# A partial 512-column unit across two steps, a weight tile's preparation moved later, and the sums of one more step by VectorE

## The chip, the core and the metric

One core of one Trainium2 chip. The metric is the device time of one execution in microseconds (us); 503.96 us is the median of three before the change. In what follows PE is TensorE, ACT is ScalarE, DVE is VectorE.

## What is computed

Attention with capped scores over 4 batches, 12 heads, 448 tokens, 64 features, then a layer with three weight matrices, an elementwise maximum and an output matrix:

```python
scores = cap * np.tanh(scale * (q @ k.T) / cap)
attn = exp(scores - max); attn = attn / (sum(attn) + 1e-09)
x = (attn @ v)                       # 1792 tokens x 768 features
h = max(max(x @ w1, x @ w2), x @ w3)
out = h @ w_out
```

All in float32. The weights arrive as 64-bit numbers and are turned into two float32r parts on the chip.

## The kernel before

**Attention.** Twelve groups of four heads, one for each step t = 0 to 11. A group has seven key chunks j. For each, PE computes `scores(t, j)` (L133, eight instructions on 64 x 64 quarters of the array), ACT applies `tanh` (L139) and `expo` (L142), and PE accumulates `values(t, j)` in the tile `av` (L151, also 64 x 64 quarters). Scores alternate between two tiles `qk`. Steps 0 to 3 are `early_step`; steps 4 to 11 are `step`; a thirteenth call ends group 11. Each engine runs its list in the order in which the functions issue it.

**Sums.** DVE adds the seven exponentials: `add` (into `s_t`), `add_aside` (chunks 3, 4 and 5 into `p_t`), `add_both`, and `add(t, 6)` at the step's end. For groups 5 to 11 (`BY_DVE`) the next step begins with `quarter_sums`: a DVE transpose (L185) and a reduction (L186) into `g_um`, then `join_sums` (L191), eight tiny PE instructions that add the parts of `g_um` by the pattern `pat`. For group 4, `sums` (L178) does the whole sum on PE instead. Then `recip` (reciprocal L199 or L202, transpose L203), `normalize` and `split_x` on DVE make the two float32r parts of x in `xx`.

**Units.** The layer's products are cut into units (n, b): weight tile n (768 x 128, six row parts `kc`) by token block b. Block 0 has 256 columns, blocks 1 to 3 have 512. A unit is 18 matmuls (L273 to L275, three for each row part) on the whole 128 x 128 array. Steps 4 to 11 take one unit each (`FILL`), in bank 0 of the tile `sm`; `empty` writes it to its place: tile 0 of a feature block by an ACT copy (L286), the others by a DVE maximum. Units of 256 columns stand in steps 4 to 6, of 512 in steps 7 to 11. All the others follow in `mlp` after attention, where PE runs products alone.

**Weights.** A weight tile is prepared by `conv(n, 0..5)` (L246 to L266), mostly on DVE; `CONV` and `PLACES` say in which step and where in it. Tile 2's pieces 3 and 4 stand at the end of step 4, piece 5 in step 5; tile 3's piece 0 is done by ACT at the end of step 7 (`SCALED`).

**One step on PE**, in order: sums or join of the group before among the first scores and values; `scores(t, 4)`, `values(t-1, 6)`, `scores(t, 5)`, the unit's products, `scores(t, 6)`, `values(t, 0)`, `values(t, 1)`, `scores(t+1, 0)`, `values(t, 2)`, `scores(t+1, 1)`, `values(t, 3)`, `scores(t+1, 2)`, and in the next step `scores(t+1, 3)`, `values(t, 4)`, `values(t, 5)`, `join_sums`. On ACT the end of a step is `tanh(t, 6)`, `expo(t, 5)` where the unit has 256 columns and `expo(t, 5)`, `tanh(t, 6)` where it has 512; then `expo(t, 6)`, the copy or ACT piece if there is one, and `tanh(t+1, 0)`.

Of the kernel before, what the change touches and what calls it, by code (L numbers as in the profile page):

```python
# [11 lines left out]
ALU = mybir.AluOpType  # L12
# [5 lines left out]
KC = DM // 128  # L18
NJ = S // 64
GB = H // 4  # L20
NG = B * GB
# [8 lines left out]
CAP_LO = 1e-6  # L30
WARM = 7

FILL = {4 + i: (i % 3, i // 3) for i in range(8)}
FILLED = (2, 2)
BY_PE = (0, 1, 2, 3)
BY_DVE = (5, 6, 7, 8, 9, 10, 11)
CONV = {0: [(0, 0), (0, 1), (0, 2), (0, 3), (0, 4), (0, 5), (1, 0), (1, 1), (1, 2), (1, 3), (1, 4)], 1: [(1, 5)],
        2: [(2, 0), (2, 1)], 3: [(2, 2)], 4: [(2, 3), (2, 4)], 5: [(2, 5)], 8: [(3, 1)], 9: [(3, 2)], 10: [(3, 3)]}
PLACES = {0: (0, 0, 0, 0, 1, 1, 1, 3, 3, 5, 5), 5: (4,), 8: (4,), 9: (4,), 10: (4,)}
EARLY = 4  # L40
SCALED = {7: 3}
LOADS = {1: 2, 6: 3, 11: 4}


# [1 line left out]
def attn_max_mlp_kernel(ctx: ExitStack, tc: tile.TileContext, first, q, k, v, wts, out):  # L46
# [11 lines left out]
    def tl(name, shape, dt=F32, pool=const):  # L58
        return pool.tile(shape, dt, name=name, tag=name)
# [4 lines left out]
    acap, sc_t, eps_f, eps_g, fl = (tl(n, [128, 1]) for n in ("acap", "sc_t", "eps_f", "eps_g", "fl"))  # L64
    fl_i = tl("fl_i", [128, 1], I32)
    ones = tl("ones", [128, 64])
    pat = tl("pat", [128, 64])
    pat_i = tl("pat_i", [128, 64], I32)
    wz = tl("wz", [128, S], F32R)

# [39 lines left out]
    def rows(i):  # L110
        return slice(64 * i, 64 * i + 64)
# [17 lines left out]
    def scores(t, j):  # L129
        ps = slot(t, j)  # L130
        for R in range(2):
            for s in range(2):
                nc.tensor.matmul(  # L133
                    ps[rows(s), R, 0:S], k_t[t % 2][rows(R), j, s, :], q_t[t % 2][rows(R), s, :],
                    start=True, stop=True, skip_group_check=True,
                )

    def tanh(t, j):
        nc.scalar.activation(out=e_of(t, j), in_=slot(t, j)[:, :, 0:S], func=AF.Tanh, scale=sc_t)  # L139

    def expo(t, j):
        nc.scalar.activation(out=e_of(t, j), in_=e_of(t, j), func=AF.Exp, scale=acap)  # L142
# [13 lines left out]
    def add(t, j, eps=None):  # L156
        s = flat(s_t[t % 2])
        if j == 1:
            nc.vector.scalar_tensor_tensor(
                out=s, in0=flat(e_of(t, 0)), scalar=eps, in1=flat(e_of(t, 1)), op0=ALU.add, op1=ALU.add  # L160
            )
        else:
            tt(nc.vector, s, s, flat(e_of(t, j)), ALU.add)
# [24 lines left out]
    def join_sums():  # L188
        for s in range(2):
            for R in range(2):  # L190
                nc.tensor.matmul(  # L191
                    sm[rows(R), s, 0:QB], pat[rows(s), :], g_um[rows(s), R * QB:R * QB + QB],
                    start=True, stop=True, skip_group_check=True,
                )

    def recip(t, by_dve=False):
        x, r = x_t[t % 2], r_t[t % 2]
        if by_dve:
            nc.vector.reciprocal(r.rearrange("p (a b) -> p a b", a=2), sm[:, :, 0:QB])  # L199
        else:  # L200
            nc.vector.transpose(out=x, in_=sm[:, :, 0:S])
            nc.vector.reciprocal(r, flat(x).rearrange("p (a b) -> p a b", b=32)[:, :, 0])  # L202
        nc.vector.transpose(  # L203
            out=flat(x).rearrange("p (a b) -> p a b", b=32), in_=r.unsqueeze(2).to_broadcast([128, 2 * QB, 32])
        )
# [62 lines left out]
    def products(n, b, ps, kcs):  # L268
        at = slice(*BLOCKS[b])
        ps = ps[:, 0:at.stop - at.start]  # L270
        for kc in kcs:
            w_h, w_l, a_h, a_l = wh[n % 3][:, kc, :], wl[n % 3][:, kc, :], xx[:, 0, kc, at], xx[:, 1, kc, at]
            nc.tensor.matmul(ps, w_h, a_h, start=(kc == 0), stop=False)  # L273
            nc.tensor.matmul(ps, w_h, a_l, start=False, stop=False)  # L274
            nc.tensor.matmul(ps, w_l, a_h, start=False, stop=(kc == KC - 1))  # L275
# [94 lines left out]
    def step(t, eps, ahead):  # L370
        last = t - 1
        if t < NG - 1:
            load_qk(t + 1)
        by_dve = last in BY_DVE
        if by_dve:
            quarter_sums(last)
        else:
            sums(last, last in BY_PE)
            recip(last)
        if t == NG:  # L380
            for j in range(4, NJ):
                values(last, j)
            ahead(range(3))
            join_sums()
            recip(last, True)
            normalize(last)
            split_x(last)
            return
        n, b = FILL[t]
        tanh(t, 1)  # L390
        expo(t, 0)
        scores(t, 3)
        if t > EARLY:
            values(last, 4)
        values(last, 5)
        if by_dve:
            join_sums()
            recip(last, True)
        tanh(t, 2)
        expo(t, 1)  # L400
        add(t, 1, eps)
        scores(t, 4)
        values(last, 6)
        normalize(last)
        tanh(t, 3)
        expo(t, 2)
        add(t, 2)
        split_x(last)
        loads(t)
        scores(t, 5)  # L410
        products(n, b, sm[:, 0, :], range(KC))
        tanh(t, 4)
        expo(t, 3)
        tanh(t, 5)
        expo(t, 4)
        add_aside(t, 4)
        scores(t, 6)
        if b:
            expo(t, 5)
            tanh(t, 6)  # L420
        else:
            tanh(t, 6)
            expo(t, 5)
        if n:
            empty(n, b, sm[:, 0, :])
        convert(t, 4)
        add_aside(t, 5)
        add_both(t)
        if not n and not b:
            empty(n, b, sm[:, 0, :])  # L430
        expo(t, 6)
        if not n and b:
            empty(n, b, sm[:, 0, :])
        if t in SCALED:
            conv(SCALED[t], 0, True)
        values(t, 0)
        values(t, 1)
        if t + 1 < NG:
            scores(t + 1, 0)
        values(t, 2)  # L440
        if t + 1 < NG:
            scores(t + 1, 1)
        if t not in BY_PE:
            add(t, 6)
        convert(t, 5)
        values(t, 3)
        if t + 1 < NG:
            tanh(t + 1, 0)
            scores(t + 1, 2)
# [77 lines left out]
    with tc.manual_schedule():  # L527
        nc.sync.dma_start(out=k_t[0][:, 0:2].rearrange("p a b c -> p (a b c)"), in_=k[0, :, 0:256])
        nc.scalar.dma_start(out=q_0[:, 0:2 * S + 1], in_=first)
        nc.scalar.dma_start(out=k_t[0][:, 2:].rearrange("p a b c -> p (a b c)"), in_=k[0, :, 256:])  # L530
        conv_load(0, nc.scalar)
        load_v(0, nc.scalar)
        conv_load(1, nc.scalar)
        nc.vector.memset(wz.bitcast(F32), 0.0)
        for _ in range(WARM):
            nc.tensor.matmul(sm[:, 0, 0:S], wz[:, 0:128], wz, start=True, stop=True)
        nc.gpsimd.memset(ones, 1.0)
        nc.gpsimd.memset(eps_g, 1e-9 / 64.0)
        nc.gpsimd.iota(pat_i, pattern=[[1, 64]], base=128, channel_multiplier=-1)
        nc.vector.tensor_single_scalar(pat_i, pat_i, 31, op=ALU.bitwise_and)  # L540
        nc.vector.tensor_single_scalar(pat, pat_i, 0, op=ALU.is_equal)
        nc.scalar.activation(out=acap, in_=cap_t, func=AF.Abs)
        nc.vector.tensor_scalar(out=fl, in0=acap, scalar1=CAP_HI, scalar2=None, op0=ALU.is_le)
        nc.vector.scalar_tensor_tensor(
            out=fl_i, in0=acap, scalar=CAP_LO, in1=fl, op0=ALU.is_ge, op1=ALU.mult
        )
        nc.vector.reciprocal(sc_t, acap)
        nc.vector.tensor_scalar_mul(sc_t, sc_t, 1.0 / float(D) ** 0.5)
        nc.scalar.activation(out=eps_f, in_=acap, func=AF.Exp, scale=-1.0)
        nc.vector.tensor_scalar_mul(eps_f, eps_f, 1e-9 / 64.0)  # L550
        scores(0, 0)
        scores(0, 1)
        tanh(0, 0)
        scores(0, 2)
        flag = nc.values_load(fl_i[0:1, 0:1], min_val=0, max_val=1)
        with tc.If(flag > 0) as br:
            load_qk(1)
            load_v(1)
            for t in range(NG + 1):
                if t < EARLY:  # L560
                    early_step(t, eps_f)
                else:
                    step(t, eps_f, lambda kcs: products(*FILLED, banks[0], kcs))
            mlp({*FILL.values()}, convs)
        outs[0] = 0
        with br.Else():
            general_attention()
            for n in range(3):
                for i in range(6):
                    conv(n, i)  # L570
                conv_load(n + 2)
            for i in range(4):
                conv(3, i)
            mlp(set(), convs)
# [49 lines left out]
```

## Time and profile before

| | |
|---|---|
| median of three executions | 503.96 us (503.28 to 504.41) |
| the profiled execution | 504.0 us, its span 502.2 us |
| mean granted TensorE clock | 0.995 |
| busy PE, DVE, ACT | 490.6, 266.4, 226.0 us |
| attention | to about 178 us of the span |

The span runs from the first to the last instruction; 1.8 us lie around it. A matmul's recorded duration overlaps the next one, so that on PE the distance from start to start is what counts.

### The profile page before, as it was taken

How to read it: one execution, taken by the hardware profiler on the slowest of the kernel's cores; microseconds unless marked ns; L12 is line 12 of the kernel's file. 1: busy time of each engine (PE TensorE's matmuls, PEld its weight loads, DVE VectorE, ACT ScalarE, POOL GpSimd, SP SyncE). 2: the span in 40 equal slices, each digit the busy share in tenths (PEclk: the TensorE clock that was granted, in tenths of full speed). 3: DMA queues.
4: the chain of work that ended last, by engine and by line, in shares of the span. 5: the costliest groups of instructions: out<-in, count | busy, mean ns of one | idle time of the engine just before them, and what ended most of it. 6: DMA issues, size and time to landing. Idle time of an engine off the chain costs nothing.

```text
span 502.2 us, 7429 instructions
## 1 busy us (share of the span) xinstructions
PE 490.6 (98%) x3207; PEld 350.1 (70%) x3207; DVE 266.4 (53%) x330; ACT 226.0 (45%) x273; POOL 0.6 (0%) x7
## 2 busy tenths in 40 slices
PE   6999999999999999999999999999999999999994
PEld 2333344454545588888888888888888888888883
DVE  4999999997898946143233323423432585222000
ACT  6999999989988602210210221121011553222110
POOL 0000000000000000000000000000000000000000
PEclk9999999999999999999999999999999999999998
DMA  8243333531324001111101301111030102233111
GB/s 331 88 174 112 112 111 111 174 104 45 111 81 158 1 0 64 63 64 63 64 5 59 125 1 63 64 63 38 27 125 1 63 2 101 89 135 127 62 74 48
DMA packets 12423, 41.44 MB, mean 83 GB/s; under 512 B 1376, under 2 KB 2528, under 8 KB 12384
## 3 DMA queue, kind: packets, MB, share of 16 engines
q1 hardware_dynamic: 11520, 37.95, 21.9%
q10 hardware_dynamic: 864, 2.95, 1.5%
q8 instruction: 27, 0.44, 0.3%
q14 instruction: 12, 0.10, 0.1%
HBM read 35.39 MB, written 5.51 MB: 81 GB/s over the span
## 4 chain that ended last, share of the span: by engine, by line
PE 85%; DVE 6%; ACT 5%; issue 2%; DMA 1%; DVEq 0%
PE qk L273 9%; PE qk L274 9%; PE qk L275 9%; PE qk L133 8%; PE sm L273 8%; PE av L151 8%; PE sm L274 7%; PE sm L275 7%; PE av L273 6%; PE av L275 6%; PE av L274 6%; ACT e_all L139 3%; DVE s_t L108 2%; ACT e_all L142 1%; ACT e_all L146 1%
## 5 line engine op out<-in xcount | busy, mean ns | idle before, releaser
L273 PE MATMUL qk<-xx,wh 128*128 128x512 f32 (+1 forms) x264 | 89.9, 340 | 0.0
L274 PE MATMUL qk<-xx,wh 128*128 128x512 f32 (+1 forms) x264 | 89.8, 340 | 0.0
L275 PE MATMUL qk<-xx,wl 128*128 128x512 f32 (+1 forms) x264 | 89.5, 339 | 0.0
L139 ACT ACTIVATE e_all<-qk,sc_t 128x896 f32<-128x896 f32 x84 | 83.6, 1014 | 11.1 <-PE qk L133 11.1
L133 PE MATMUL qk<-q,k_t 64*64 64x448 f32 x672 | 77.5, 547 | 2.7 <-ACT e_all L139 2.2
L151 PE MATMUL av<-e_all,v_t 64*64 64x448 f32 x672 | 72.7, 536 | 0.0
L262 ACT CAST wh<-cw 128x768 fp32r<-128x768 f32 x21 | 17.6, 836 | 116.2 <-DVE cw L258 116.2
L273 PE MATMUL sm<-xx,wh 128*128 128x512 f32 (+1 forms) x180 | 69.2, 384 | 0.0
L274 PE MATMUL sm<-xx,wh 128*128 128x512 f32 (+1 forms) x180 | 68.4, 380 | 0.0
L275 PE MATMUL sm<-xx,wl 128*128 128x512 f32 (+1 forms) x180 | 68.2, 379 | 0.0
L142 ACT ACTIVATE e_all<-e_all,acap 128x896 f32<-128x896 f32 x60 | 62.0, 1047 | 0.2
L273 PEld LDWEIGHTS qk<-xx,wh 128*128 128x128 f32 x264 | 50.2, 190 | 6.3 <-issue 0.7
L275 PEld LDWEIGHTS qk<-xx,wl 128*128 128x128 f32 x264 | 50.1, 190 | 5.6
L274 PEld LDWEIGHTS qk<-xx,wh 128*128 128x128 f32 x264 | 50.2, 190 | 5.3
L151 PEld LDWEIGHTS av<-e_all,v_t 64*64 64x64 f32 x672 | 25.9, 133 | 37.2 <-issue 34.1
L275 PE MATMUL av<-xx,wl 128*128 128x512 f32 x132 | 51.4, 390 | 0.0
L273 PE MATMUL av<-xx,wh 128*128 128x512 f32 x132 | 51.4, 390 | 0.0
L274 PE MATMUL av<-xx,wh 128*128 128x512 f32 x132 | 51.4, 390 | 0.0
L133 PEld LDWEIGHTS qk<-q,k_t 64*64 64x64 f32 x672 | 23.8, 134 | 38.5 <-issue 17.7
L108 DVE TENSOR_TENSOR wl<-cw,wh 128x768 fp32r<-128x768 f32 x24 | 22.9, 956 | 41.6 <-ACT wh L262 36.2
L273 PEld LDWEIGHTS sm<-xx,wh 128*128 128x128 f32 x180 | 33.8, 188 | 11.8 <-DVE x_t L203 4.2
L108 DVE TENSOR_TENSOR e_all<-e_all,qk 128x256 f32<-128x256 f32 (+1 forms) x20 | 11.1, 555 | 52.7 <-PE qk L275 52.7
(77 smaller groups left out, 486.1 us busy)
## 6 DMA issues: line engine op xcount, KB each, us to landing
wd<-in_wts_dram SPq DMA_DIRECT2D x22, 768.0 KB, 4.2
k_t<-in_k_dram SPq DMA_DIRECT2D x11, 448.0 KB, 3.4
q<-in_q_dram SPq DMA_DIRECT2D x11, 448.0 KB, 5.0
v_t<-in_v_dram SPq DMA_DIRECT2D x11, 448.0 KB, 3.3
wd<-in_wts_dram ACTq DMA_DIRECT2D x2, 768.0 KB, 6.9
out_dram<-q SPq DMA_DIRECT2D x6, 256.0 KB, 2.0
out_dram<-s_t SPq DMA_DIRECT2D x6, 256.0 KB, 2.0
out_dram<-x_t SPq DMA_DIRECT2D x5, 256.0 KB, 2.0
```

What stands on the lines that cost most here:

```text
L108: eng.tensor_tensor(out=out, in0=in0, in1=in1, op=op)
L133: nc.tensor.matmul(ps[rows(s), R, 0:S], k_t[t % 2][rows(R), j, s, :], q_t[t % 2][rows(R), s, :], start=True, stop=True, skip_group_check=True,
L139: nc.scalar.activation(out=e_of(t, j), in_=slot(t, j)[:, :, 0:S], func=AF.Tanh, scale=sc_t)
L142: nc.scalar.activation(out=e_of(t, j), in_=e_of(t, j), func=AF.Exp, scale=acap)
L146: nc.scalar.activation(out=e, in_=e, func=AF.Exp, scale=acap)
L151: nc.tensor.matmul(av[rows(R), s, 0:S], v_t[t % 2][rows(s), j, R, :], e_of(t, j)[rows(s), R, :], start=(j == 0), stop=(j == NJ - 1), skip_ ...
L262: nc.scalar.copy(out=h, in_=d)
L273: nc.tensor.matmul(ps, w_h, a_h, start=(kc == 0), stop=False)
L274: nc.tensor.matmul(ps, w_h, a_l, start=False, stop=False)
L275: nc.tensor.matmul(ps, w_l, a_h, start=False, stop=(kc == KC - 1))
```

## The change

Tile 2's unit (2, 0) goes from step 6 to step 8. Step 6 takes row parts 0 to 3 of unit (0, 1), whose sums stay in bank 0 of `sm`; step 7 adds the last two parts and takes the whole of unit (1, 1) in bank 1. Steps 9 to 11 are as before. Tile 2's pieces 3 to 5 all go to step 7, tile 3's pieces one step later each. Group 4's sums go by `quarter_sums` and `join_sums`. `join_sums` writes bank 1 alone; `pat` becomes a pair of 128-row patterns with zeros in the other half, so that each of its matmuls contracts 128 rows into 64 columns. In the steps of `SHORT` the `recip` stands behind `add(t, 1)`, and `tanh(t, 6)` goes ahead of `expo(t, 5)`.

```diff
+FILL = {4: [(0, 0, ALL, 0)], 5: [(1, 0, ALL, 0)], 6: [(0, 1, range(4), 0)], 7: [(0, 1, range(4, KC), 0), (1, 1, ALL, 1)],
+        8: [(2, 0, ALL, 0)], 9: [(2, 1, ALL, 0)], 10: [(0, 2, ALL, 0)], 11: [(1, 2, ALL, 0)]}
+SHORT = (4, 5, 6, 8)
-BY_DVE = (5, 6, 7, 8, 9, 10, 11)
+BY_DVE = range(4, NG)
-        2: [(2, 0), (2, 1)], 3: [(2, 2)], 4: [(2, 3), (2, 4)], 5: [(2, 5)], 8: [(3, 1)], 9: [(3, 2)], 10: [(3, 3)]}
+        2: [(2, 0), (2, 1)], 3: [(2, 2)], 7: [(2, 3), (2, 4), (2, 5)], 9: [(3, 1)], 10: [(3, 2)], 11: [(3, 3)]}
-SCALED = {7: 3}
+SCALED = {8: 3}
...
-    pat = tl("pat", [128, 64])
+    pat = tl("pat", [128, 2, 64])
...
-                    sm[rows(R), s, 0:QB], pat[rows(s), :], g_um[rows(s), R * QB:R * QB + QB],
+                    sm[rows(R), 1, s * QB:s * QB + QB], pat[:, s, :], g_um[:, R * QB:R * QB + QB],
...
-            nc.vector.reciprocal(r.rearrange("p (a b) -> p a b", a=2), sm[:, :, 0:QB])
+            nc.vector.reciprocal(r, sm[:, 1, 0:2 * QB])
...
+        units = [(n, b, kcs, sm[:, i, :]) for n, b, kcs, i in FILL[t]]
+        short = t in SHORT
...
+        def empty_units(by_act):
+            for n, b, kcs, ps in units:
+                if kcs.stop == KC and by_act == (n == 0):
+                    empty(n, b, ps)
...
             join_sums()
-            recip(last, True)
+            if not short:
+                recip(last, True)
         tanh(t, 2)
         expo(t, 1)
         add(t, 1, eps)
+        if by_dve and short:
+            recip(last, True)
...
-        products(n, b, sm[:, 0, :], range(KC))
+        for n, b, kcs, ps in units:
+            products(n, b, ps, kcs)
...
-        if b:
+        if short:
+            tanh(t, 6)
+            expo(t, 5)
+        else:
+            if len(units) > 1:
+                empty_units(True)
             expo(t, 5)
             tanh(t, 6)
-        else:
-            tanh(t, 6)
-            expo(t, 5)
-        if n:
-            empty(n, b, sm[:, 0, :])
+        empty_units(False)
         convert(t, 4)
         add_aside(t, 5)
         add_both(t)
-        if not n and not b:
-            empty(n, b, sm[:, 0, :])
-        expo(t, 6)
-        if not n and b:
-            empty(n, b, sm[:, 0, :])
+        if short:
+            empty_units(True)
+            expo(t, 6)
+        else:
+            expo(t, 6)
+            if len(units) == 1:
+                empty_units(True)
...
-        nc.vector.tensor_single_scalar(pat, pat_i, 0, op=ALU.is_equal)
+        nc.vector.memset(pat, 0.0)
+        for i in range(2):
+            nc.vector.tensor_single_scalar(pat[rows(i), i, :], pat_i[rows(i)], 0, op=ALU.is_equal)
```

## Rows read from the trace of the kernel before

**Rows 1.** The page, part 1: busy us, share of the span, instructions.

```profile
PE 490.6 (98%) x3207; PEld 350.1 (70%) x3207; DVE 266.4 (53%) x330; ACT 226.0 (45%) x273; POOL 0.6 (0%) x7
```

**Rows 2.** Timeline of PE, steps 5 and 6: start us, us, what, count, idle before.

```profile
79.34 0.98 PE L133 MATMUL qk<-q,k_t 64*64 64x448 f32 x8
...
88.09 0.30 PE L191 MATMUL sm<-g_um,pat 64*64 64x14 f32 x8 [0.25 <-DVE g_um L186]
88.23 0.96 PE L133 MATMUL qk<-q,k_t 64*64 64x448 f32 x8
...
90.62 0.39 PE L273 MATMUL sm<-xx,wh 128*128 128x256 f32 x1
90.84 0.28 PE L274 MATMUL sm<-xx,wh 128*128 128x256 f32 x1
...
92.75 0.28 PE L275 MATMUL sm<-xx,wl 128*128 128x256 f32 x1
92.96 0.98 PE L133 MATMUL qk<-q,k_t 64*64 64x448 f32 x8
```

**Rows 3.** Timeline of ACT at the end of step 5.

```profile
80.39 1.01 ACT L139 ACTIVATE e_all<-qk,sc_t 128x896 f32<-128x896 f32 x1 [0.99 <-PE qk L133]
81.29 1.96 ACT L142 ACTIVATE e_all<-e_all,acap 128x896 f32<-128x896 f32 x2
83.16 2.00 ACT L139 ACTIVATE e_all<-qk,sc_t 128x896 f32<-128x896 f32 x2
```

**Rows 4.** Timeline of DVE, end of step 4 and end of step 5.

```profile
71.44 0.95 DVE L258 SCALAR_TENSOR_TENSOR cw<-wd,cw 128x768 int32<-128x768 int32 x1
72.42 0.56 DVE L264 CAST wh<-cw 128x768 fp32r<-128x768 f32 x1
...
81.47 0.95 DVE L108 TENSOR_TENSOR wl<-cw,wh 128x768 fp32r<-128x768 f32 x1
82.36 1.09 DVE L108 TENSOR_TENSOR p_t<-p_t,e_all 128x896 f32<-128x896 f32 x1
...
85.80 1.11 DVE L185 STREAM_TRANSPOSE x_t<-s_t 128x896 f32<-128x896 f32 x1
86.95 1.09 DVE L186 TENSOR_REDUCE g_um<-x_t 128x28 f32<-128x896 f32 x1
```

**Rows 5.** Timeline of PE, end of step 4 and the sums of group 4.

```profile
65.09 0.98 PE L133 MATMUL qk<-q,k_t 64*64 64x448 f32 x8
...
71.58 0.98 PE L178 MATMUL sm<-s_t,ones 64*64 64x448 f32 x8 [0.24 <-DVE s_t L108]
72.38 0.93 PE L133 MATMUL qk<-q,k_t 64*64 64x448 f32 x8
```

**Rows 6.** Timeline of PE, steps 7 to 9.

```profile
104.28 0.50 PE L273 MATMUL sm<-xx,wh 128*128 128x512 f32 x1
...
108.58 0.98 PE L133 MATMUL qk<-q,k_t 64*64 64x448 f32 x8
...
117.19 0.25 PE L191 MATMUL sm<-g_um,pat 64*64 64x14 f32 x8
...
124.01 0.98 PE L133 MATMUL qk<-q,k_t 64*64 64x448 f32 x8
...
132.33 0.25 PE L191 MATMUL sm<-g_um,pat 64*64 64x14 f32 x8
132.42 0.96 PE L133 MATMUL qk<-q,k_t 64*64 64x448 f32 x8
```

**Rows 7.** Timeline of ACT, end of step 7.

```profile
112.09 0.94 ACT L246 ACTIVATE cw<-wd 128x768 f32<-128x768 f32 x1
112.93 1.90 ACT L139 ACTIVATE e_all<-qk,sc_t 128x896 f32<-128x896 f32 x2
```

**Rows 8.** Timeline of DVE, the maximum that empties the unit of step 8.

```profile
124.69 0.68 DVE L108 TENSOR_TENSOR m<-m,sm 128x512 f32<-128x512 f32 x1
```

**Rows 9.** Timeline of DVE at the start of the kernel.

```profile
5.03 0.15 DVE L543 TENSOR_SCALAR fl<-acap 128x1 f32<-128x1 f32 x1 [3.42 <-ACT acap L542]
```

More of the change, by code (lines that the diff above doesn't have):

```diff
@@ L31 @@
 WARM = 7
-FILL = {4 + i: (i % 3, i // 3) for i in range(8)}
+ALL = range(KC)
+FILL = {4: [(0, 0, ALL, 0)], 5: [(1, 0, ALL, 0)], 6: [(0, 1, range(4), 0)], 7: [(0, 1, range(4, KC), 0), (1, 1, ALL, 1)],
+        8: [(2, 0, ALL, 0)], 9: [(2, 1, ALL, 0)], 10: [(0, 2, ALL, 0)], 11: [(1, 2, ALL, 0)]}
+SHORT = (4, 5, 6, 8)
 FILLED = (2, 2)
 BY_PE = (0, 1, 2, 3)
-BY_DVE = (5, 6, 7, 8, 9, 10, 11)
+BY_DVE = range(4, NG)
 CONV = {0: [(0, 0), (0, 1), (0, 2), (0, 3), (0, 4), (0, 5), (1, 0), (1, 1), (1, 2), (1, 3), (1, 4)], 1: [(1, 5)],
-        2: [(2, 0), (2, 1)], 3: [(2, 2)], 4: [(2, 3), (2, 4)], 5: [(2, 5)], 8: [(3, 1)], 9: [(3, 2)], 10: [(3, 3)]}
-PLACES = {0: (0, 0, 0, 0, 1, 1, 1, 3, 3, 5, 5), 5: (4,), 8: (4,), 9: (4,), 10: (4,)}
+        2: [(2, 0), (2, 1)], 3: [(2, 2)], 7: [(2, 3), (2, 4), (2, 5)], 9: [(3, 1)], 10: [(3, 2)], 11: [(3, 3)]}
+PLACES = {0: (0, 0, 0, 0, 1, 1, 1, 3, 3, 5, 5), 7: (4, 4, 4), 9: (4,), 10: (4,), 11: (4,)}
 EARLY = 4
-SCALED = {7: 3}
+SCALED = {8: 3}
 LOADS = {1: 2, 6: 3, 11: 4}
@@ L388, in step @@
             return
-        n, b = FILL[t]
+        units = [(n, b, kcs, sm[:, i, :]) for n, b, kcs, i in FILL[t]]
[4 more added lines that the diff above has]
+                    empty(n, b, ps)
         tanh(t, 1)
@@ L563, in attn_max_mlp_kernel @@
                     step(t, eps_f, lambda kcs: products(*FILLED, banks[0], kcs))
-            mlp({*FILL.values()}, convs)
+            mlp({unit[:2] for units in FILL.values() for unit in units}, convs)
         outs[0] = 0
```

## The prediction

> **What bounds the kernel now.** I read the page first: PE is busy for 98% of the span [rows 1]. After attention PE runs products without a break, and the change leaves the set of units as it is. So the time changes only by what PE does or waits for up to the last of the changed steps, and the view to read is the timeline of PE there, start to start. I call S(t) the start of `scores(t, 6)`, right behind a step's products, and J(t) the start of the join in step t. Two distances make up the whole of attention's second part.
>
> From S to the next join. PE itself has eleven groups of scores and values there. In a step where it waits for nothing this is 124.01 to 132.33 = 8.32 us [rows 6], 0.755 a group. Behind a 256-column unit it is 79.34 to 88.09 = 8.75 us [rows 2]: 0.43 us of waiting for the DVE reduction, 0.25 of it as shown idle. What sets those 8.75 us is read on the other two engines. `tanh(5, 6)` waits for the scores and starts at S + 1.05; the two exponentials follow at S + 1.95 [rows 3]; DVE's `add_aside(5)` starts at S + 3.02, as the first of them ends; then come `add_both`, `add(6)`, the transpose and the reduction, which starts at S + 7.61 and lasts 1.09 [rows 4]; the join starts 0.05 us behind it. So this is a loop: products, scores, tanh, exp, four additions and a reduction, join, and the products again behind it.
>
> From the join to the next S: 88.09 to 92.96 = 4.87 us with a 256-column unit [rows 2], and 117.19 to 124.01 = 6.82 with a 512-column one [rows 6]. The units alone take 90.62 to 92.96 = 2.34 and 104.28 to 108.58 = 4.30. In the small unit a matmul takes (92.75 - 90.84)/16 = 0.119 us [rows 2]; the large one adds (4.30 - 2.34)/18 = 0.109 to that, so 0.228.
>
> Before, the loop holds PE at three places (steps 5, 6 and 7, each behind a 256-column unit), and at a fourth, step 8, by ACT: 108.58 to 117.19 is 8.61, 0.29 over 8.32, because ACT's copy and weight piece push `tanh(8, 0)` to 112.93, S + 4.35 [rows 6, 7].
>
> **The change, part by part.** First with the join at its old price.
>
> Group 4's sums. They start at 71.58, behind a wait for the last addition, and the next scores follow 0.80 later [rows 5]. The join in their place is reached by the loop: J(5) = 65.09 + 8.75 = 73.84, S(5) = 73.84 + 4.87 = 78.71 instead of 79.34. That is 0.63 us won; DVE pays a reduction more (1.09) and has tile 2's pieces 3 and 4 less (0.98 and 0.56 [rows 4]).
>
> Weight pieces out of steps 4 and 5. These 0.98 + 0.56 + 0.89 us of DVE gain nothing by leaving: in step 5 the piece ends just as the exponential does, and `add_aside(5)` starts at S + 3.02 with or without it. In the changed steps 5, 6 and 8 that addition still waits for `expo(t, 5)`, which still stands behind `tanh(t, 6)`. `recip` behind `add(t, 1)` fills DVE's wait for the join, on an engine that is not late there: value 0. If it were, the cover is the wait of `add_aside(5)`.
>
> Step 6: twelve matmuls of 0.228 instead of eighteen of 0.119, 0.59 more, in the loop and so not hidden. J(6) = 78.71 + 8.75 = 87.46; S(6) = 87.46 + 4.87 + 0.59 = 92.92 (before 92.96). J(7) = 92.92 + 8.75 = 101.67.
>
> Step 7: six more matmuls, 1.37 us. S(7) = 101.67 + 6.82 + 1.37 = 109.86. ACT copies the finished unit ahead of S, where it has nothing else to do. DVE comes to the maximum of (1, 1) about 7.5 us behind the join (117.19 to 124.69 in step 8 [rows 6, 8]), but the products now end 8.2 us behind it. So DVE waits there, and behind it stand the maximum (0.68), the three weight pieces (0.98 + 0.56 + 0.89) and `add_aside(5)`. With the maximum at about S + 0.1 (an estimate) the addition starts at S + 3.1 to 3.3; from its start to the join it is 82.36 to 88.09 = 5.73 [rows 2, 4], so J(8) = S(7) + 8.83 to 9.0. I take 8.9: 118.76. The pieces have used up the slack that a long step gave DVE, and the wait at the join is there again.
>
> Step 8 is now a short one: S(8) = 118.76 + 4.87 = 123.63 (before 124.01). At its end ACT has tanh, two exponentials and tile 3's piece: `tanh(9, 0)` at S + 3.82 [rows 2, 3] + 0.84 [rows 7] = S + 4.66, which is 0.31 later than the 4.35 that gave 8.61 before. J(9) = 123.63 + 8.92 = 132.55, against 132.33. From there on the units and orders are the old ones.
>
> So with a join at the old price: **+0.22 us**. 0.63 us from the sums are given back by one more short step, and by the pieces in step 7.
>
> The join. It has the same eight instructions, now over 128 rows into 64 columns, so two at a time instead of four. No 128 x 64 instruction is in the trace. From below, 0 a join: it has no less to do. From above: each of eight weight loads laid open, as the first of a unit is (90.62 to 90.84 is 0.22, 0.10 over the 0.119), with an entry of 0.14 and an exit of 0.09: 1.0 us against 0.09, so about 0.9 a join. Where I put it between: the nearest rows are the borders between 64 x 64 quarters and the whole array. Entering costs 88.23 to 90.62 = 2.39 against three groups of 0.75 (0.755 without the exit that is in the 8.32), so 0.14; leaving costs 92.75 to 92.96 = 0.21 against 0.119, so 0.09 [rows 2]. The body took 0.14 us after a wait (88.09 to 88.23) and 0.09 without one (132.33 to 132.42 [rows 6]); two at a time I double 0.14 to 0.28. Behind a wait the entry is hidden: +0.14 + 0.09 = 0.23. Without one: 0.14 + 0.28 + 0.09 - 0.09 = 0.42. Steps 5 to 8 wait (4 x 0.23 = 0.92), steps 9 to 11 do not (3 x 0.42 = 1.26): **+2.18 us**. The thirteenth call's join stands between whole-array products in both kernels, at 0.
>
> The rows show a border that costs PE 0.14 and 0.09 us. The Trainium skill (TensorEngine Tiling (Array Packing), Tiling Modes, Key Properties) says that changing the tiling mode, not just the tile, drains TensorE, and lists 128 x 64 as a mode beside 64 x 64; by it the join has both borders, as taken. Were only the body dearer (0.14 each, no border), the join's term would be 7 x 0.14 = 0.98 and the whole +1.2.
>
> Elsewhere: `pat`'s extra memset and comparison stand in DVE's 3.42 us of idleness at the start [rows 9], so 0. Tile 3's pieces come a step later each; one is new in step 11 (below 1 us), ahead of the last group's reduction, and its cover is the nine products that PE does before the thirteenth join (9 x 0.228 = 2.05). No DMA moves in any queue; tile 2's loaded data are read until step 7, and the next load into that buffer is issued in step 11. Products no longer have to wait for the reciprocal's read of bank 0, but they start over 2 us behind the join: 0.
>
> Sum: 504.0 + 0.22 + 2.18 = **506.4 us**, from the profiled execution (502.2 + 1.8), which is the median within 0.04.
>
> **The rivals.**
>
> *The join keeps its price.* Then the kernel is at 504.2. For it: the borders seen are to the full array, not to half of it. Against it: four row quarters still have to be joined. Chance 0.23, with cases in which the join costs less than 0.1 us more.
>
> *The waits at the joins go.* DVE has less to do in steps 4 to 6 and its reciprocal is out of the way. If `add_aside(5)` started 0.43 us earlier, at S + 2.6 or before, and step 7's pieces fitted in ahead of S, the joins would come at S + 8.32: three times 0.43 less, and 0.58 and 0.60 less in steps 8 and 9, 2.47 us together. With the join at its old price that gives 504.0 + 0.22 - 2.47 = 501.8; with my join, whose entry would then be hidden nowhere (7 x 0.42 = 2.94), 504.7. For it: DVE is without a pause through step 5. Against it: rows 3 and 4 put the addition right at the end of the exponential, and the order on ACT is the old one. Chance 0.10, most of it with a cheap join.
>
> *The join is much dearer*, its loads laid open: 0.9 a join, 7 x 0.9 + 0.22 = 510.5. Chance 0.07.
>
> **How the numbers follow.** My forecast, with a join 0.1 to 0.6 dearer, has 0.60: 505.0 to 508.4 by 0.22 + 7 x 0.1 and 0.22 + 7 x 0.6, each to a tenth or two. The range takes in the join at its old price with half a microsecond for the chain's rounding, 503.6 to 508.2. About 0.2% (1.0 us) is what a measurement of this kernel can tell from no change. Faster than that 0.09 (0.08 of it the second rival); within it 0.27 (0.21 the join at its old price, the rest the lower edge of the forecast and the waits gone under a dear join); slower 0.64.
>
> **What would show it.** S(5) about 0.6 us earlier plus one join; a wait of 0.4 us at the joins of steps 5 to 8; S(6) to the next join still 8.75; DVE idle ahead of the maximum of (1, 1); the join to the next scores 0.3 to 0.4 us instead of 0.09 to 0.14, and steps 9 to 11 at 15.5 us each from S to S instead of 15.15. The forecast is wrong if those steps keep 15.15, or if joins come at S + 8.3 behind the short steps.

## The result

The changed kernel takes 507.86 us (median of 16 executions), the kernel before 504.9 (16 executions beside them): a ratio of 1.0057, 95% interval 1.0045 to 1.0069, or 2.3 to 3.5 us slower. The forecast was 2.4 us slower than the kernel before. The forecast's 506.4 us lies 1.5 us below the measured time: 0.9 of that is its starting point (504.0, where the kernel before takes 504.9 over 16 executions), the rest is in what the change adds.

The timeline of PE in the changed kernel, the S and J of each step, here with the idle time ahead of a join (lines are shifted by three: L133 is L136, the join L194):

```profile
65.10 0.98 PE L136 MATMUL qk<-q,k_t 64*64 64x448 f32 x8
...
73.86 0.41 PE L194 MATMUL sm<-g_um,pat 128*64 128x14 f32 x8 [0.23 <-DVE g_um L189]
74.19 0.98 PE L136 MATMUL qk<-q,k_t 64*64 64x448 f32 x8
...
78.96 0.98 PE L136 MATMUL qk<-q,k_t 64*64 64x448 f32 x8
...
87.72 0.41 PE L194 MATMUL sm<-g_um,pat 128*64 128x14 f32 x8 [0.26 <-DVE g_um L189]
...
93.42 0.98 PE L136 MATMUL qk<-q,k_t 64*64 64x448 f32 x8
...
102.18 0.41 PE L194 MATMUL sm<-g_um,pat 128*64 128x14 f32 x8 [0.25 <-DVE g_um L189]
...
110.60 0.98 PE L136 MATMUL qk<-q,k_t 64*64 64x448 f32 x8
...
120.11 0.41 PE L194 MATMUL sm<-g_um,pat 128*64 128x14 f32 x8 [1.01 <-DVE g_um L189]
...
125.21 0.98 PE L136 MATMUL qk<-q,k_t 64*64 64x448 f32 x8
...
134.23 0.41 PE L194 MATMUL sm<-g_um,pat 128*64 128x14 f32 x8
134.57 0.98 PE L136 MATMUL qk<-q,k_t 64*64 64x448 f32 x8
...
141.29 0.98 PE L136 MATMUL qk<-q,k_t 64*64 64x448 f32 x8
...
149.72 0.41 PE L194 MATMUL sm<-g_um,pat 128*64 128x14 f32 x8
...
156.78 0.98 PE L136 MATMUL qk<-q,k_t 64*64 64x448 f32 x8
...
180.75 0.41 PE L194 MATMUL sm<-g_um,pat 128*64 128x14 f32 x8
```

What to see: the join is followed by the next scores 0.33 to 0.34 us later, with a wait ahead of it (73.86) or without (134.23); before it was 0.14 and 0.09 [rows 2, 6]. From S to S with nothing but PE's own work, 141.29 to 156.78, is 15.49 us, against 124.01 [rows 6] to 139.16 = 15.15 in the kernel before. And J(8) stands 9.51 us behind S(7), the longest of them.

The same timeline of the kernel before has these two lines, S(9) and the last join:

```profile
139.16 0.98 PE L133 MATMUL qk<-q,k_t 64*64 64x448 f32 x8
...
177.92 0.30 PE L191 MATMUL sm<-g_um,pat 64*64 64x14 f32 x8
```

From S(4) to the last join it is 115.65 us; in the kernel before 65.09 [rows 5] to 177.92 = 112.83. That 2.82 is nearly the whole of the difference of the spans (505.4 - 502.2 = 3.2); 0.1 more is the time from the last join to the next products (0.34 against 0.24), and 0.3 lies behind PE's last matmul.

When S(4) comes differs from profile to profile (64.5 to 67.7 us in those of this study). The waits at the start differ, and in five profiles (e2, e3, e6, e9, e11) the granted clock fell towards the lower of its two levels (1.2 instead of 2.4 GHz), to 0.50 to 0.88 in the stretch from 12 to 16 us; it fell behind a wait of PE for ACT of 1.59 us, which the kernel before has too, without the fall. From 20 us on it is 0.99 or 1.00 in all. So below each kernel's distance from S(4) to its last join is compared, besides its time. Stretches that a variant leaves alone agree from profile to profile to 0.05 us.

| stretch | before | after | difference | forecast |
|---|---|---|---|---|
| S(4) to S(5) | 14.25 | 13.86 | -0.39 | -0.40 |
| S(5) to S(7) | 29.24 | 31.64 | +2.40 | +2.37 |
| S(7) to J(8) | 8.61 | 9.51 | +0.90 | +0.29 |
| J(8) to S(8) | 6.82 | 5.10 | -1.72 | -1.72 |
| S(8) to J(9) | 8.32 | 9.02 | +0.70 | +0.74 |
| J(9) to the last join | 45.59 | 46.52 | +0.93 | +1.12 |
| together | 112.83 | 115.65 | +2.82 | +2.40 |

The forecast column is the prediction's own numbers, the joins' 0.23 and 0.42 put where they fall: of the 0.42 of step 9, the entry (0.14) lies ahead of J(9). One stretch was missed, S(7) to J(8). What holds it is read on ACT and on DVE. The timeline of ACT in step 7 of the changed kernel (L289 is the copy of unit (0, 1)):

```profile
106.43 1.06 ACT L145 ACTIVATE e_all<-e_all,acap 128x896 f32<-128x896 f32 x1
110.71 0.58 ACT L289 COPY m<-sm 128x512 f32<-128x512 f32 x1 [3.23 <-PE sm L278]
111.19 1.04 ACT L145 ACTIVATE e_all<-e_all,acap 128x896 f32<-128x896 f32 x1
112.13 1.00 ACT L142 ACTIVATE e_all<-qk,sc_t 128x896 f32<-128x896 f32 x1
```

The timeline of DVE there:

```profile
108.73 1.08 DVE L111 TENSOR_TENSOR p_t<-e_all 128x896 f32<-128x896 f32 x1
111.33 0.69 DVE L111 TENSOR_TENSOR m<-m,sm 128x512 f32<-128x512 f32 x1 [1.51 <-ACT m L289]
111.93 0.95 DVE L261 SCALAR_TENSOR_TENSOR cw<-wd,cw 128x768 int32<-128x768 int32 x1
112.92 0.56 DVE L267 CAST wh<-cw 128x768 fp32r<-128x768 f32 x1
113.51 0.96 DVE L111 TENSOR_TENSOR wl<-cw,wh 128x768 fp32r<-128x768 f32 x1
114.39 1.08 DVE L111 TENSOR_TENSOR p_t<-p_t,e_all 128x896 f32<-128x896 f32 x1
...
118.97 1.08 DVE L189 TENSOR_REDUCE g_um<-x_t 128x28 f32<-128x896 f32 x1
```

Unit (0, 1) is complete six matmuls into the step's products, by 106.6, but its copy starts at 110.71, behind all 24. The maximum of (1, 1) needs the copied values, since both go to the same place, so it waits for ACT and starts at S + 0.73 instead of about S + 0.1. Behind it stand the three weight pieces, and `add_aside(5)` starts at S + 3.79.

### The profile page after: what moved, and what is told of

Read it like the earlier page. It is cut to its first block, busy times and chain, and to the rows that moved or that the text cites. A ratio compares the mean times of both kernels' runs of the same rounds, so it can differ in the third digit from the quotient of the medians.

```text
span 505.4 us, 7427 instructions
## 1 busy us (share of the span) xinstructions
PE 492.3 (97%) x3207; PEld 350.6 (69%) x3207; DVE 268.2 (53%) x333; ACT 225.9 (45%) x273; POOL 0.6 (0%) x7
## 4 chain that ended last, share of the span: by engine, by line
PE 84%; ACT 6%; DVE 6%; issue 1%; DMA 1%; DVEq 0%
PE qk L276 9%; PE qk L277 9%; PE qk L278 9%; PE sm L276 8%; PE qk L136 8%; PE sm L277 8%; PE sm L278 8%; PE av L154 6%; PE av L277 6%; PE av L276 6%; PE av L278 6%; ACT e_all L142 4%; DVE s_t L111 2%; ACT e_all L145 1%; ACT e_all L149 1%
## 5 line engine op out<-in xcount | busy, mean ns | idle before, releaser
L136 PE MATMUL qk<-q,k_t 64*64 64x448 f32 x672 | 77.4, 547 | 2.9 <-ACT e_all L142 2.4
L136 PEld LDWEIGHTS qk<-q,k_t 64*64 64x64 f32 x672 | 23.6, 133 | 38.7 <-issue 19.3
```

The lines of the kernel that those rows point to most:

```text
L136: nc.tensor.matmul(ps[rows(s), R, 0:S], k_t[t % 2][rows(R), j, s, :], q_t[t % 2][rows(R), s, :], start=True, stop=True, skip_group_check=True,
```

## The experiments

Each time is a median, each ratio that of its executions to those of the kernel before on the same chip, with its 95% interval; "from S(4)" is the distance to the last join in the profile, 112.83 before and 115.65 in the changed kernel. An interval reaches 0.5 to 0.9 us to either side, so differences of a few tenths are read from the profiles alone, one for each variant.

**e1: the join alone, in the kernel before.**

```diff
-    sm[rows(R), s, 0:QB], pat[rows(s), :], g_um[rows(s), R * QB:R * QB + QB],
+    sm[rows(R), 1, s * QB:s * QB + QB], pat[:, s, :], g_um[:, R * QB:R * QB + QB],
...
-            nc.vector.reciprocal(r.rearrange("p (a b) -> p a b", a=2), sm[:, :, 0:QB])
+            nc.vector.reciprocal(r, sm[:, 1, 0:2 * QB])
...
```

> The kernel before with one part of the change: the join over 128 rows into bank 1, the reciprocal reading it there. Theory (the join's array mode is the dear part): the join to the next scores takes 0.34 us instead of 0.09 to 0.14; behind a wait (steps 6 and 7) 0.2 us more each, without one (steps 8 to 11) 0.25 behind the join and 0.11 ahead of it, so 15.5 us from S to S in steps 9 to 11; 0.1 in the last join. Sum 2 x 0.2 + 4 x 0.35 + 0.1 = 1.9 us over the kernel before. Rival (the new placing of units and pieces costs the time): within 0.3 us of before.

507.27 us, ratio 1.0047 (1.0029 to 1.0065); 114.65 from S(4), 1.82 us more. The timeline of PE in steps 8 to 10:

```profile
118.99 0.41 PE L191 MATMUL sm<-g_um,pat 128*64 128x14 f32 x8
119.33 0.98 PE L133 MATMUL qk<-q,k_t 64*64 64x448 f32 x8
...
126.05 0.98 PE L133 MATMUL qk<-q,k_t 64*64 64x448 f32 x8
...
134.47 0.41 PE L191 MATMUL sm<-g_um,pat 128*64 128x14 f32 x8
...
141.54 0.98 PE L133 MATMUL qk<-q,k_t 64*64 64x448 f32 x8
```

126.05 to 134.47 is 8.42 us, 0.10 over the 8.32 of [rows 6]: the entry. 134.47 to 141.54 is 7.07 against 6.83: 0.24 for body and exit. No unit, piece or order was touched, so the join's form alone makes a slower kernel. The rival is out as the whole cause.

**e2: the old join in the changed kernel**, in all steps but 7.

```diff
+        if quarters:
+            ...
+            sm[rows(R), s, 0:QB], pat[rows(s), s, :], g_um[rows(s), R * QB:R * QB + QB],
...
-            join_sums()
+            join_sums(t != 7)
```

> The changed kernel with the old join on 64 x 64 quarters in both banks, in all steps but step 7, where bank 0 is taken. Theory (the join's array mode): 0.2 us less in steps 5, 6 and 8, 0.35 less in steps 9 to 11, 0.1 in the last, 1.8 us less than the changed kernel, which leaves about 1.1 us over before. Rival (units and pieces): within 0.3 us of the changed kernel.

505.9 us, ratio 1.0021 (1.0007 to 1.0034); 113.90 from S(4), 1.75 less than the changed kernel. Put in or taken out, the join is worth the same. What is left, 1.07 us over before, is in the placing of the work, but for about 0.2 us of the join of step 7, which keeps its new form here.

**e3: the pieces ahead of the maximum in step 7.**

```diff
-        empty_units(False)
-        convert(t, 4)
+        if len(units) > 1:
+            convert(t, 4)
+            empty_units(False)
+        else:
+            empty_units(False)
+            convert(t, 4)
```

> The changed kernel with tile 2's three pieces ahead of the maximum of (1, 1) in step 7, in the time in which DVE waits for it. Theory (DVE's maximum and the pieces behind it hold the join of step 8): the join of step 8 comes at S + 8.4 instead of 9.51, 1.1 us less in all. Rival (the late products or ACT's late tanh hold it, the order on DVE does not matter): within 0.2 us of the changed kernel.

506.88 us, ratio 1.0050 (1.0034 to 1.0066); 114.55 from S(4), 1.10 less than the changed kernel. The timeline of PE:

```profile
111.54 0.98 PE L136 MATMUL qk<-q,k_t 64*64 64x448 f32 x8
...
119.97 0.41 PE L194 MATMUL sm<-g_um,pat 128*64 128x14 f32 x8
```

8.43 us, which is 8.32 and the join's entry: the wait is gone although ACT's copy is as late as it was. DVE's order held that join. The ratio is only 0.0007 below the changed kernel's, within both intervals: the 1.1 us are read in the profile, not in the time.

**e4: the exponential first in step 6.**

```diff
-        if short:
+        if short and t != 6:
             tanh(t, 6)
             expo(t, 5)
```

> The changed kernel with expo(6, 5) ahead of tanh(6, 6) in step 6, where ACT is idle for 1.46 us before that tanh. Theory (the loop from S to the join runs over the exponential): the join of step 7 comes at S + 8.4 instead of 8.76, 0.3 us less. Rival (DVE's own work sets it): 8.76 as it is, no change.

507.26 us, ratio 1.0057 (1.0038 to 1.0075), too coarse for 0.3 us; the profile decides. 115.33 from S(4), 0.32 less, and the timeline of PE has

```profile
93.18 0.98 PE L136 MATMUL qk<-q,k_t 64*64 64x448 f32 x8
...
101.61 0.41 PE L194 MATMUL sm<-g_um,pat 128*64 128x14 f32 x8
```

8.43 instead of 8.76. So the wait behind this short step came over the exponential. In the changed kernel DVE stood idle for 1.47 us ahead of that addition, waiting for it.

**e5: the tile in two.**

```diff
-    sm = tl("sm", [128, 2, 512], pool=psum)
+    sm = ring("sm", 2, [128, 512], pool=psum)
...
-            nc.vector.transpose(out=x, in_=sm[:, :, 0:S])
+            for i in range(2):
+                nc.vector.transpose(out=x[:, i, :], in_=sm[i][:, 0:S])
...
```

> The changed kernel with the tile sm declared as two tiles of one bank each, so that the copy of unit (0, 1) no longer waits for the last write to the other bank (the sums of steps 0 to 3 are transposed in two halves for it). Theory (the copy of step 7 waits for all 24 products since both banks are one tile, and the maximum of (1, 1) waits for the copy): the copy starts 3.2 us earlier, the maximum at S + 0.15 instead of 0.73, the join of step 8 at S + 8.93 instead of 9.51, 0.6 us less. Rival (DVE's maximum waits for the products as I had it, and the pieces alone make the 9.51): 9.51 as it is.

505.88 us, ratio 1.0020 (1.0009 to 1.0032); 115.15 from S(4), 0.50 less. The timelines of ACT, DVE and PE in step 7:

```profile
106.81 0.60 ACT L290 COPY m<-sm 128x512 f32<-128x512 f32 x1
```

```profile
110.24 0.69 DVE L111 TENSOR_TENSOR m<-m,sm 128x512 f32<-128x512 f32 x1 [0.97 <-PE sm L279]
```

```profile
110.06 0.98 PE L136 MATMUL qk<-q,k_t 64*64 64x448 f32 x8
...
119.03 0.41 PE L194 MATMUL sm<-g_um,pat 128*64 128x14 f32 x8 [0.47 <-DVE g_um L189]
```

The copy runs early, the maximum waits for the products alone and starts at S + 0.18, and the join is 8.97 us behind S: the prediction's 8.9. Of the 0.61 us that it missed, 0.54 were this wait of one bank for the other. The whole came out better than these joins explain: from the last output's issue (498.38) to the end of the span (502.5) it was 4.1 us, where the kernel before takes 5.7 (496.51 to 502.2) and the changed kernel 6.0. e11 asks about that.

**e6: ACT's piece in step 7.**

```diff
-SCALED = {8: 3}
+SCALED = {}
...
             if len(units) > 1:
+                conv(3, 0, True)
                 empty_units(True)
```

> The changed kernel with tile 3's first piece done by ACT in step 7, ahead of the copy, where ACT is idle for 3.2 us, instead of at the end of step 8. Theory (the piece pushes tanh(9, 0) and PE waits for it): the join of step 9 at S + 8.76, the loop's distance, instead of 9.02, 0.26 us less. Rival (the distance of 9.02 is the loop's plus the join's entry): 9.02 as it is.

507.92 us, ratio 1.0047 (1.0030 to 1.0065); 115.40 from S(4), 0.25 less. The timeline of PE:

```profile
127.76 0.98 PE L136 MATMUL qk<-q,k_t 64*64 64x448 f32 x8
...
136.54 0.41 PE L194 MATMUL sm<-g_um,pat 128*64 128x14 f32 x8 [0.28 <-DVE g_um L189]
```

S(8) to J(9) is 8.78, and the join now waits for DVE's reduction (0.28 us shown idle) where it had waited for nothing. As the theory has it.

**e7: group 4's sums by PE.**

```diff
-BY_DVE = range(4, NG)
+BY_DVE = range(5, NG)
```

> The changed kernel with group 4's sums by PE as before. Theory: S(4) to S(5) is 14.25 us as in the kernel before instead of 13.86, 0.39 us more: what the new sums win is 0.63 less the dearer join. Rival (the sums are hidden behind DVE's work either way): 0.

507.91 us, ratio 1.0064 (1.0045 to 1.0083); 116.08 from S(4), 0.43 more, with S(4) to S(5) 14.26 (65.14 to 79.40). That part of the change does win what was computed, by the profile.

**e8: all of these together**: e2, e3 and e6, and `tanh(t, 6)` ahead of `expo(t, 5)` in step 4 alone.

```diff
-        if short:
+        if t == 4:
             tanh(t, 6)
             expo(t, 5)
```

> The changed kernel with the old join but in step 7, the pieces ahead of the maximum, the exponential ahead of tanh(t, 6) in steps 5, 6 and 8, and ACT's piece in step 7. Theory (the terms add up): joins of steps 6, 8 and 9 at S + 8.32 and of step 7 at S + 8.43; from S(4) to the last join 111.4 us, against 112.83 before and 115.65 in the changed kernel: 1.4 us faster than before. Rival (with the waits gone, DVE's own work holds the joins at S + 8.7): 112.5 or more, no faster than before by what can be measured.

504.52 us, ratio 0.9985 (0.9973 to 0.9997); 112.09 from S(4): 0.74 us less than before, half of the 1.4 expected. J(7) and J(8) came as expected, at S + 8.42 and S + 8.32; J(6) came at S + 8.53 and J(9) at S + 8.84. The timeline of DVE in step 8:

```profile
119.39 1.15 DVE L162 SCALAR_TENSOR_TENSOR s_t<-e_all,eps_f 128x896 f32<-128x896 f32 x1 [0.75 <-ACT e_all L145]
...
127.04 1.08 DVE L111 TENSOR_TENSOR p_t<-p_t,e_all 128x896 f32<-128x896 f32 x1
...
131.63 1.09 DVE L189 TENSOR_REDUCE g_um<-x_t 128x28 f32<-128x896 f32 x1
```

From 119.39 to the reduction it has no idle time, nor in step 5 from the unit's maximum to the reduction. With the waits behind `expo(t, 5)` gone, DVE's own list is what the join waits for: the rival's mechanism, at two joins of four. In step 8 that list itself starts late, by 0.75 us of waiting for `expo(8, 1)`.

**e9: the exponential first in the kernel before**, in steps 5 and 6.

```diff
-        if b:
+        if t != 4:
             expo(t, 5)
             tanh(t, 6)
```

> The kernel before with the exponential ahead of tanh(t, 6) in steps 5 and 6 too. Theory (the loop holds the join at S + 8.75 behind step 6, while in step 5 DVE's own work with tile 2's last piece would hold it there in any case): the join of step 7 at S + 8.32, the join of step 6 still at S + 8.75; 0.4 us less in all. Rival (ACT's order alone): both at S + 8.32, 0.85 us less. Other rival (neither): no change.

504.69 us, ratio 0.9995 (0.9983 to 1.0006); 112.65 from S(4), 0.18 less than before instead of 0.4. J(6) came at S + 8.72 (80.31 to 89.03), as expected, but J(7) at S + 8.65 (93.91 to 102.56): a miss. The timeline of DVE in step 6:

```profile
96.50 0.41 DVE L108 TENSOR_TENSOR m<-m,sm 128x256 f32<-128x256 f32 x1
96.83 1.08 DVE L108 TENSOR_TENSOR p_t<-p_t,e_all 128x896 f32<-128x896 f32 x1
...
101.42 1.09 DVE L186 TENSOR_REDUCE g_um<-x_t 128x28 f32<-128x896 f32 x1
```

`add_aside(5)` follows the maximum at once, at S + 2.92, only 0.1 before the exponential used to let it start. Two chains stood there within 0.1 us of each other, ACT's and DVE's own, and the trace of before showed only the later one. In e4 the same move gave 0.33: there `add_aside(5)` comes at S + 1.64, since the changed kernel has no maximum in step 6, its reciprocal does not wait for the join, and the step's products take 0.6 us longer.

**e10: e8 with the tile in two.**

```diff
-            nc.vector.reciprocal(r.rearrange("p (a b) -> p a b", a=2), sm[:, :, 0:QB])
+            for i in range(2):
+                nc.vector.reciprocal(r[:, QB * i:QB * i + QB], sm[i][:, 0:QB])
...
```

> The kernel of e8_all_mended with sm as two tiles, so two reciprocals behind each quarter join. Theory (there DVE's own work holds the joins of steps 6 and 9; in step 8 it is late since ACT's copy in step 7 delayed the exponential for add(8, 1)): the copy runs early, DVE no longer waits for that exponential, and the join of step 9 comes at S + 8.5 to 8.6 instead of 8.84; the second reciprocal is 0.3 us more on DVE ahead of the join of step 6, S + 8.8 instead of 8.53. Sum about 0. Rival (the copy's wait costs PE nothing any more): 0.3 to 0.6 us slower.

503.29 us, ratio 0.9973 (0.9961 to 0.9985), the fastest of all. But both of its joins were forecast wrong: 112.11 from S(4) is e8's 112.09, J(9) at S + 8.87, J(6) at S + 8.53. The two reciprocals of 14 columns took 0.35 us together (one of 28 takes 0.33), and `add(8, 1)` still waited 0.78 us for its exponential though the copy was early; so the copy had not been what delayed it. Its lead over e8 lies outside the changed steps: in the profiles S(4) came 1.4 us earlier, which differs from profile to profile, and behind the last output, where e5's lead lay, it was 4.7 us instead of e8's 5.8.

**e11: the tile in two in the kernel before.**

```diff
-    sm = tl("sm", [128, 2, 512], pool=psum)
+    sm = ring("sm", 2, [128, 512], pool=psum)
...
```

> The kernel before with sm as two tiles of one bank each (two reciprocals, two halves of a transpose), nothing else. It tells where e5 and e10 won what their joins do not show: from the last output's issue to the end of the span they took 4.1 and 4.7 us, all the others 5.7. Theory (the declaration as two tiles shortens that end): 4.1 to 4.7 us here too, the joins as before, 1.0 to 1.5 us less in all. Rival (chance of two profiles): 5.7 us, and the whole within 0.4 us of before.

505.24 us, ratio 1.0001 (0.9991 to 1.0012); 5.8 us from the last output's issue (497.84) to the end of the span (503.6). The theory falls: the declaration alone doesn't shorten the end. What differs in e5 and e10 is what SyncE's queue waits for at the last line of the kernel (L619 before). In the eleven other profiles 1.9 to 2.1 us of it are for ACT's queue and 0.5 to 0.8 for DVE's; in e5 and e10 none are for these two, and those for PE's queue are 1.3 and 1.7 instead of 0.3. Added up, the waits there are 4.7 us before and 3.0 in e5, 4.9 in e8 and 3.6 in e10, which is the difference of the ends to 0.2 us. Why it waits for ACT's queue in the others and not in these two stays open.

## Why the prediction was right, and where it was off

**The bound and the loop** were read rightly: joins at S + 8.76 behind steps 4 to 6 (73.86, 87.72, 102.18), as the 8.75 of [rows 2] said, and the products inside the loop, so that step 6's larger share was not hidden. e4 shows that in step 6 of the changed kernel the loop runs over the exponential. For the kernel before, the statement that DVE was not late was true by 0.1 us only (e9).

**Group 4's sums**: -0.39 against -0.40, and e7 puts back 0.43.

**The join**: 0.23 behind a wait, as taken (J(5) to S(5) 5.10 against 4.87). Without a wait 0.345 where I took 0.42: the entry cost 0.10 to 0.11, not 0.14, and body with exit 0.24, not 0.28. e1 and e2 show 1.82 and 1.75 us for the join's form, about two thirds of the change; e2 leaves the join of step 7 out of that. The rule of the Trainium skill (TensorEngine Tiling (Array Packing), Tiling Modes, Key Properties), that changing the mode drains TensorE, agrees with the 0.10 us ahead of a join that waits for nothing; the runs do not separate drain, weight loads and matmuls in the 0.24 behind it.

**Step 7** is the step that failed: "DVE waits there, and behind it stand the maximum, the three weight pieces and `add_aside(5)`" held, but not "with the maximum at about S + 0.1". It was S + 0.73, because the copy of the finished unit does not go "ahead of S" as I wrote: it waited for the products in the other bank of the same tile (e5), and the maximum for the copy. J(8) came 0.61 us later behind S(7) than the 8.9 forecast. e3 shows that with the pieces ahead of the maximum even the late copy costs PE nothing.

**ACT's piece in step 8** was sized well: 9.02 against 8.92, the rest being the join's entry; e6 takes it out.

**The total.** That the sum of the stretches is only 0.4 us off (2.82 against 2.40) is in part luck: the 0.61 missed in step 7 is partly offset by 0.19 of the later joins, which were taken too dear.

**The rivals.** The join did not keep its price (e1). The waits did not go; e8 shows that with the order mended two of the four joins came as early as that rival had them. The very dear join did not occur.

## What to carry to other kernels

A tiny step can cost much by its array mode: here eight matmuls of 14 columns over 128 rows took 0.2 to 0.35 us more per step than in 64 x 64 quarters, and that was most of the loss. Only the 0.10 us of the entry are seen by themselves. Work moved into a step's slack must also stand in the right place of its engine's list: the same pieces cost 1.1 us behind a waiting instruction and nothing ahead of it (e3). Before a wait is called removable, add up the engine's own list beside it; a second chain 0.1 us shorter doesn't show until the first is gone.

## What the runs showed of the hardware that was not expected

In the changed kernel a read of one bank of a two-bank tile waited 3.2 us for the matmuls into the other bank; declared as two tiles it did not (e5). There ACT read one bank (106.81 to 107.41) while the matmuls wrote the other, so the wait lay in how the program orders the two engines and not in the memory.

The join in 128 x 64 mode took the same 0.33 to 0.34 us to the next scores whether PE had waited ahead of it or not, where the quarters took 0.14 and 0.09.
